# Softmax weights of the later head pairs: turned on VectorE before they go through DRAM

## The chip, the cores and the metric

One core of a Trainium2 chip. The metric is the device time of one execution in microseconds (us). Three executions of the kernel before took 894.09, 897.22 and 897.65 us (median 897.22). A fourth one was recorded by the profiler; it took 890.54 us, and all rows below are of it.

## The reference

Local and strided attention over 8 batches of 8 heads, 576 positions and 64 values a head, then layer norm and a two-layer network of width 512 and 2048:

```
mask_local   = (rel >= 0) & (rel < 32)                    # heads 0 to 3, rel = i - j
mask_strided = (rel >= 0) & (j % 32 == i % 32)            # heads 4 to 7
attn = softmax(where(mask, q k^T / 8, -1e9));   x = (attn v) as (8, 576, 512)
xn   = (x - mean) / sqrt(var + 1e-6) * g_ln
out  = x + relu(xn w_ch1) w_ch2
```

All of it is float32.

## The kernel before, in words

**Pairs.** Two heads of one batch are a pair; a batch has four pairs, by turns a local one (18 blocks of 32 queries against 64 keys) and a strided one (11 blocks of up to 54 positions that share a residue). Pairs are numbered 0 to 31: 0 to 7 are the first two batches, 8 to 11 the third. "Later pairs" are 8 to 31; of them 12 are local and 12 strided.

**The network.** Chunks of 512 tokens go through 16 steps each. A step is `ffn1` (12 products 512 wide into the bank `ph`, L800), then `hh` on ScalarE (L806) and `hl` on VectorE (L811), and `ffn2` of the step before (two halves of 6 products, L825). `ph` is one bank, so the next step's `ffn1` waits for `hl`. Steps are numbered n from 8 up; 8 to 23 are chunk 1, 24 to 31 the second half of chunk 0, from 32 on the other chunks.

**Attention between the steps.** A *visit* of pair i (`scores_and_values`, L611) stands between the network's products: on TensorE the values of pair i and then the scores of pair i+2, both in small tiles of the array (L656); on VectorE the scaling of the values into `xo` (L664), the mask and the row maximum; on GpSimd the subtraction (L485); on ScalarE the exponential (L490), which leaves the weights in `sm`. There is one `sm` for local and one for strided pairs. `x_store` then sends `xo` to DRAM. `sums` (L720) adds up the weights' rows on VectorE.

**Turning the weights.** The values need the weights transposed. Pairs 8 to 12 get that on TensorE: `turn_weights` (L701), 5 or 6 transposes of 128x128 and a copy by ScalarE. Pairs 13 to 31 get it by way of DRAM: `weights_out` (L676) stores `sm`, `weights_in` (L682) fetches it back through `to_blocks` (L696) in four transfers whose runs are 32 values long, and `turn_blocks` (L709) turns the 32x32 blocks on VectorE.

**Order.** All is issued in program order on each engine; SyncE issues nearly all transfers, in order. The start, until the first network steps run, is the hand-written list `ORDER`; there `K.n.w` is n idle products of width w on TensorE. From step 16 to 31 `early_steps` says by a letter and a pair what stands where: v visit, r sums, w turn_weights, o weights_out, p weights_in, x and y the fetching and turning of `x`, l the loading of v, t the turning of q and k, a and s rows of chunk 0. The fractions are places in a step: -0.25 ahead of `ffn1`, 0 after it, 0.25 between the halves of `ffn2`, 0.5 after them. From step 32 on the generator `visits` (L1097) does three parts for each pair, on three of every four steps.

Of the kernel before, what the change touches and what calls it, by code (L numbers as in the profile page):

```python
# [18 lines left out]

ORDER = """  # L20
L.a L.b L.c R.a/DVE L.X0 T.a K.1.512 K.1.256 L.Y0 R.b/POOL C.ka/ACT C.qa/DVE L.X1 T.b R.c/POOL S.a L.d C.qb/DVE
C.kb/ACT M.a w0.sc0 T.c w0.lo0 Z.a/DVE S.b K.1.256 C.qc/ACT L.va w0.mg0 U.a C.kc/ACT w0.sg0 M.b S.c w0.lo1 w0.bg
w0.sc1 Z.b/DVE E.a w0.mg1 U.b w1.sc0 L.vb P.a K.2.512 w0.sg1 M.c R.d/POOL w1.lo0 E.b w1.mg0 w0.cs T.d G.a w1.sg0
P.b w1.bg C.qd/DVE C.kd/ACT L.Y1 L.vc G.b Z.c/DVE w0.cm S.d w0.ce U.c V.a M.d L.X2 w0.hi0 w1.cs O.a E.c V.b L.Y2
w0.lw0 O.b w1.sc1 X.a w1.cm H.a L.a1 Z.d/DVE w1.lo1 X.b D.c/POOL Y.a H.b w1.mg1 P.c K.1.512 L.vd Y.b G.c U.d
w2.sc0 w1.sg1 w0.hi1 V.c w1.ce E.d w0.lw1 F1.0.b O.c w2.lo0 P.d L.b1 w2.sc1 w2.mg0 R.a1/POOL G.d X.c w2.sg0 H.c
K.1.512 T.a1 w2.lo1 w2.bg Y.c L.X3 w2.mg1 L.va1 C.ka1/ACT V.d w2.cs w2.sg1 F1.0.a C.qa1/ACT O.d w2.hi1 S.a1 L.Y3
w1.hi0 R.b1/POOL X.d M.a1 L.c1 w1.lw0 H.d Z.a1/DVE T.b1 U.a1 Y.d F1.1.b F1.1.a C.qb1/ACT C.kb1/DVE E.a1 w3.lo0
w3.sc0 D.a1/POOL F1.0.d w3.mg0 S.b1 w1.hi1 w3.sg0 w2.cm L.X4 P.a1 M.b1 w3.lo1 w3.bg F1.1.d L.vb1 G.a1 w2.ce
w3.cs w3.sc1 Z.b1/DVE V.a1 w2.hi0 w3.mg1 U.b1 F1.0.c O.a1 w3.cm F1.1.c w2.lw0 E.b1 L.Y4 w3.ce X.a1 L.X5 P.b1  # L30
# [13 lines left out]
def kernel(  # L44
# [14 lines left out]
    P = 128  # L59
# [132 lines left out]
    xd_l = [dram.tile([S, DM // 2], F32, name=f"xdl{b}") for b in range(B)]  # L192
    xd_s = [dram.tile([2 * NS * GS, DM // 2], F32, name=f"xds{b}") for b in range(B)]

    wd = [dram.tile([NS * P, P], F32, name=f"wd{i}") for i in range(2)]

    w1b, w2b = w1.bitcast(U32), w2.bitcast(U32)

# [412 lines left out]
    def scores_and_values(pv, p):  # L611

        one = p or pv
        n, last = one.nt, one.nt - 1
        slots = bank(f"sv{one.id}").rearrange("p (h r x) -> p h r x", h=2, x=SLOT)
        of_head = slots.shape[2]
        first_key = int(not one.local)
        vals = slots[:, :, n:2 * n] if pv else None
        keys = slots[:, :, first_key:first_key + last], slots[:, :, (first_key + last) % n]

        def middle(h, r):
            return of_head > CH // SLOT and (of_head * h + r) * SLOT // CH == 1

        passes = [[], []]
        places = [[] for _ in range(n)]
        for i, ((t, c), m) in enumerate(blocks(one)):
            places[t].append((i, c, m))
        for h in range(2):
            r = slice(64 * h, 64 * h + 64)
            if pv:  # L630
                rows = slice(64 * h, 64 * h + (64 if pv.local else GS))
                for t in sorted(range(n), key=lambda t: not middle(0, n + t)):
                    passes[h] += [
                        (vals[m * c:m * (c + 1), h, t], pv.pt[rows, t, m * c:m * (c + 1)],
                         pv.v[rows, i, 0:D], (64 * h, m * c), middle(h, n + t))
                        for i, c, m in places[t]]
            if p:
                w = 64 if p.local else GS
                step = STR if p.local else GS
                for t in sorted(range(n), key=lambda t: middle(1, (first_key + t) % n)):  # L640
                    to = keys[0][:, :, t] if t < last else keys[1]
                    passes[h] += [
                        (to[m * c:m * (c + 1), h, 0:w], p.qt[r, step * i:step * i + m],
                         p.kt[r, step * i:step * i + w], (64 * h, m * c),
                         middle(h, (first_key + t) % n))
                        for i, c, m in places[t]]
        written = [None, None]
        for both in zip(*passes):
            for h, (to, at, by, pos, shared) in enumerate(both):
                if shared and h and written[0] and not written[1]:  # L650
                    tc.add_manual_dep(
                        nc.tensor.nop().ins, written[0],
                        mybir.DependencyInfo(
                            mybir.DependencyClass.Sync, mybir.DependencyReason.DATA),
                        reason="both heads write the middle bank")
                ins = nc.tensor.matmul(  # L656
                    to, at, by, start=True, stop=True, tile_position=pos).ins
                if shared:
                    written[h] = ins.name
        if pv:  # L660
            xo = smp.tile([P, NS, 2, D], F32, tag="xo", name=f"xo{pv.id}")
            xot = xo.rearrange("p t h d -> p h t d")
            for rows, t0, t1 in ((P, 0, last), (64, last, n)):
                nc.vector.tensor_tensor(  # L664
                    out=xot[0:rows, :, t0:t1], in0=vals[0:rows, :, t0:t1],
                    in1=pv.den[0:rows, :, t0:t1].unsqueeze(3).broadcast_to([rows, 2, t1 - t0, D]),
                    op=ALU.mult)
            pv.xov = xo.rearrange("p t h d -> p t (h d)")
        if p:
            p.s_max(w, [(P, 0, last, keys[0][:, :, :, 0:w]),  # L670
                        (64, last, n, keys[1][0:64, :, 0:w].unsqueeze(2))])
            p.s_most(nc.vector.reduce_max)
            p.s_sub()
            p.s_act()

    def weights_out(p):  # L676

        nc.sync.dma_start(
            wd[int(p.local)].rearrange("(t p) x -> p t x", p=P)[:, 0:p.nt],
            p.sm[:, 0:p.nt].rearrange("p t h x -> p t (h x)"))  # L680

    def weights_in(p):  # L682

        p.pt = p.sm.rearrange("p t h x -> p t (h x)")
        p.sp = p.pt[:, 0:p.nt].rearrange("p t x -> p (t x)")
        to_blocks(p.sp, wd[int(p.local)][0:p.nt * P].rearrange("(j c) x -> c j x", c=32))

    def x_in(px):

# [8 lines left out]
            r = slice(32 * g, 32 * g + 32)  # L698
            nc.sync.dma_start(dst[r].rearrange("p (j e) -> p j e", e=32), src[:, :, r])

    def turn_weights(p):  # L701

        ps = bank(f"pp{p.id}")
        p.pt = p.sm.rearrange("p t h x -> p t (h x)")
        for t in range(p.nt):
            nc.tensor.transpose(ps[:, P * t:P * (t + 1)], p.pt[:, t], ident)  # L706
        nc.scalar.copy(out=p.pt[:, 0:p.nt].rearrange("p t x -> p (t x)"), in_=ps[:, 0:P * p.nt])

    def turn_blocks(px, p):  # L709

        if px:
            nc.vector.transpose(px.sx, px.sx)
            xh, xl = (t[:, px.h0 // 2, :] for t in x_t(px.b))
            nc.scalar.activation(out=xh, in_=px.sx, func=AF.Copy)
        if p:
            nc.vector.transpose(p.sp, p.sp)
        if px:
            nc.vector.tensor_tensor(out=xl, in0=px.sx, in1=xh.bitcast(F32), op=ALU.subtract)  # L718

    def sums(p):  # L720
        if p:
# [334 lines left out]
    def turn():  # L1056
        while todo:
            i = todo.pop()
            pairs[i].t_piece()
            if 2 * NHP <= i + 1 < NP:  # L1060
                pairs[i + 1].load_half(0)
                if i < 3 * NHP + 3:
                    pairs[i + 1].load_half(1)
# [4 lines left out]
    def visit(i):  # L1068
# [4 lines left out]
            turned(i + 3)  # L1073

    early_steps = {
# [5 lines left out]

    def early_step(n):
        stages = {"t": lambda p: p.t_piece(), "r": sums, "l": lambda p: p.load_v(), "x": x_in,
                  "w": turn_weights, "o": weights_out, "y": lambda p: turn_blocks(p, None), "p": weights_in}
        for word in early_steps.get(n, "").split():
            i = int(word[1:])
            if word[0] in "as":
# [9 lines left out]
    def visits():  # L1097

        for i in range(3 * NHP, NP):
            p, scored = pair(i + 1), pair(i + 2)  # L1100
            px = pairs[i] if pairs[i].b + 1 < B else None
            if p:
                weights_in(p)
            visit(i)
            if px:
                x_in(px)
            yield
            if i + 2 < NP:
                pairs[i + 2].load_v()
            yield  # L1110
            turn_blocks(px, p)
            sums(scored)
            if scored:
                weights_out(scored)
            if i + 4 < NP:
                pairs[i + 4].load_half(1, nc.scalar)
            yield

    late, two, h_last = {}, [], {}
    quarter = [slice(P * i, P * (i + 1)) for i in range(NT)]  # L1120
# [279 lines left out]
    for n, (r, f) in enumerate(steps):  # L1400
# [34 lines left out]
        early_step(n + 0.5)  # L1435
        if f == r.f0:
            prev[0].close()
        if old:
            old.column_mean()
            old.centred()  # L1440
# [80 lines left out]
```

## Time and profile before

| | before |
|---|---|
| median of three runs | 897.22 us (894.09 to 897.65) |
| profiled execution | 890.54 us, span 888.7 us |
| TensorE busy | 874.2 us (98%) |
| weight loads of TensorE | 715.2 us (80%) |
| VectorE, ScalarE, GpSimd busy | 454.2, 238.7, 238.5 us |
| granted TensorE clock, mean | 1.000 |

The profiled execution is 1.84 us longer than its span, which runs from the first instruction to the last. Matmuls overlap in the records: the distance of two starts is what one costs, not its duration.

### The profile page before, as it was taken

How to read it: one execution, taken by the hardware profiler on the slowest of the kernel's cores; microseconds unless marked ns; L12 is line 12 of the kernel's file. 1: busy time of each engine (PE TensorE's matmuls, PEld its weight loads, DVE VectorE, ACT ScalarE, POOL GpSimd, SP SyncE). 2: the span in 40 equal slices, each digit the busy share in tenths (PEclk: the TensorE clock that was granted, in tenths of full speed). 3: DMA queues.
4: the chain of work that ended last, by engine and by line, in shares of the span. 5: the costliest groups of instructions: out<-in, count | busy, mean ns of one | idle time of the engine just before them, and what ended most of it. 6: DMA issues, size and time to landing. Idle time of an engine off the chain costs nothing.

```text
span 888.7 us, 18483 instructions
## 1 busy us (share of the span) xinstructions
PE 874.2 (98%) x7425; PEld 715.2 (80%) x7425; DVE 454.2 (51%) x833; ACT 238.7 (27%) x431; POOL 238.5 (27%) x293
## 2 busy tenths in 40 slices
PE   7899999999999999999999999999999999999998
PEld 4678888888888888888888888878888788888886
DVE  5897476676554456445544555455543763333300
ACT  4765474212111111111111111111112543333200
POOL 6777286210000010000000000001000567676000
PEclk9999999999999999999999999999999999999999
DMA  9988880566676565657565657566532000001200
GB/s 212 227 200 249 215 247 1 123 143 148 117 165 123 103 128 132 118 100 126 129 137 113 119 106 155 112 122 129 140 91 80 13 32 28 1 1 46 95 26 24
DMA packets 339421, 101.70 MB, mean 114 GB/s; under 512 B 278160, under 2 KB 330248, under 8 KB 339336
## 3 DMA queue, kind: packets, MB, share of 16 engines
q1 hardware_dynamic: 300520, 95.28, 48.0%
q10 hardware_dynamic: 38816, 5.25, 3.6%
q8 instruction: 58, 0.95, 0.5%
q14 instruction: 27, 0.22, 0.1%
HBM read 73.42 MB, written 27.06 MB: 113 GB/s over the span
## 4 chain that ended last, share of the span: by engine, by line
PE 93%; DMA 4%; SPq 1%; DVE 1%; ACT 1%; issue 0%; POOL 0%; POOLq 0%; DVEq 0%; ACTq 0%
PE po L825 44%; PE ph L800 33%; PE u L1284 5%; PE sv L656 4%; PE v L1284 2%; DMA rows<-in_k_dram 2%; DMA v_l<-in_v_dram 1%; PE c L1284 1%; SPq L345 1%; DMA s<-in_moe_w_ch_dram 1%; SPq L356 0%; DMA v_s<-in_v_dram 0%; PE cm L267 0%; PE pp L706 0%; DVE xr L1151 0%
## 5 line engine op out<-in xcount | busy, mean ns | idle before, releaser
L825 PE MATMUL po<-w,hh 128*128 128x512 f32 x1024 | 320.5, 394 | 1.2 <-issue 0.8
L800 PE MATMUL ph<-xh,w 128*128 128x512 f32 x880 | 290.7, 391 | 0.0
L825 PEld LDWEIGHTS po<-w,hh 128*128 128x128 f32 x1024 | 189.1, 188 | 41.0 <-issue 1.0
L811 DVE SCALAR_TENSOR_TENSOR hl<-ph,hh 128x512 fp32r<-128x512 f32 x112 | 77.2, 690 | 257.5 <-ACT hh L806 257.2
L825 PE MATMUL po<-w,hl 128*128 128x512 f32 x512 | 199.6, 390 | 0.0
L800 PEld LDWEIGHTS ph<-xh,w 128*128 128x128 f32 x880 | 165.2, 188 | 34.2
L800 PE MATMUL ph<-xl,w 128*128 128x512 f32 x440 | 171.2, 389 | 0.0
L806 ACT ACTIVATE hh<-ph 128x512 fp32r<-128x512 f32 x112 | 66.7, 596 | 309.8 <-PE ph L800 284.4
L485 POOL TENSOR_TENSOR sm<-sm,mx 128x640 f32<-128x640 f32 (+1 forms) x32 | 40.6, 1269 | 343.6 <-DVE mx L481 331.8
L825 PEld LDWEIGHTS po<-w,hl 128*128 128x128 f32 x512 | 96.1, 188 | 20.7 <-issue 0.4
L800 PEld LDWEIGHTS ph<-xl,w 128*128 128x128 f32 x440 | 82.7, 188 | 16.9 <-DVE xl L718 0.2
L490 ACT ACTIVATE sm<-sm 128x640 f32<-128x640 f32 (+1 forms) x32 | 23.7, 742 | 125.3 <-POOL sm L485 125.3
L767 POOL TENSOR_TENSOR rs<-rs,mhalf 128x1 f32<-128x1 f32 x28 | 15.3, 549 | 100.8 <-DVE rs L766 94.5
L825 PE MATMUL po<-w,h 128*128 128x512 f32 x186 | 42.3, 389 | 0.0
L1151 POOL TENSOR_TENSOR sr<-sr,w 128x256 f32<-128x256 f32 x48 | 40.2, 838 | 3.8
L825 PEld LDWEIGHTS po<-w,h 128*128 128x128 f32 x186 | 34.9, 188 | 7.2
L1151 POOL TENSOR_TENSOR s<-sr,s 128x256 fp32r<-128x256 f32 x32 | 24.7, 799 | 25.5 <-ACT s L1270 25.5
L236 DVE SCALAR_TENSOR_TENSOR p<-s,p 128x512 uint32<-128x512 uint32 x32 | 22.0, 687 | 13.1 <-ACT p L232 11.2
L481 DVE TENSOR_REDUCE mx<-sm 128x10 f32<-128x640 f32 (+1 forms) x32 | 26.3, 823 | 1.9
L1151 DVE TENSOR_TENSOR x<-po,x 128x512 f32<-128x512 f32 x8 | 5.3, 688 | 39.6 <-PE po L825 29.9
L664 DVE TENSOR_TENSOR xo<-sv,den 64x128 f32<-64x128 f32 (+2 forms) x48 | 22.7, 515 | 4.5 <-PE sv L656 4.1
L566 DVE TENSOR_REDUCE den<-sm 128x10 f32<-128x640 f32 (+1 forms) x24 | 19.5, 811 | 7.8 <-ACT sm L490 7.8
(193 smaller groups left out, 974.2 us busy)
## 6 DMA issues: line engine op xcount, KB each, us to landing
s<-in_moe_w_ch_dram SPq DMA_DIRECT2D x32, 512.0 KB
out_dram<-x SPq DMA_DIRECT2D x32, 256.0 KB
raw<-in_q_dram SPq DMA_DIRECT2D x104, 72.0 KB
v_l<-in_v_dram SPq DMA_DIRECT2D x32, 144.0 KB
raw<-in_k_dram ACTq DMA_DIRECT2D x64, 72.0 KB
x<-xdl SPq DMA_DIRECT2D x34, 128.0 KB
x<-xds SPq DMA_DIRECT2D x34, 128.0 KB
xdl<-xo SPq DMA_DIRECT2D x16, 256.0 KB
```

Source lines behind the costliest of these rows:

```text
L236: nc.vector.scalar_tensor_tensor(out=self.p[i], in0=self.bits(i), scalar=3, in1=self.p[i], op0=ALU.logical_shift_left, op1=ALU.bitwise_or)
L481: engine(self.mx[:, :, 0:nt], self.smv, axis=AX.X)
L485: nc.gpsimd.tensor_tensor(out=sm, in0=sm, in1=mx[:, :, 0:nt].unsqueeze(3).broadcast_to([P, 2, nt, w]), op=ALU.subtract)
L490: nc.scalar.activation(out=self.smv, in_=self.smv, func=AF.Exp, scale=SCALE)
L656: ins = nc.tensor.matmul(to, at, by, start=True, stop=True, tile_position=pos).ins
L664: nc.vector.tensor_tensor(out=xot[0:rows, :, t0:t1], in0=vals[0:rows, :, t0:t1], in1=pv.den[0:rows, :, t0:t1].unsqueeze(3).broadcast_to([r ...
L800: nc.tensor.matmul(ph, w[:, cc], x[:, cc, :], start=(n + k == 0), stop=(n == NCC - 1 and k == 2))
L806: nc.scalar.activation(out=hh, in_=ph, func=AF.Relu)
L811: nc.vector.scalar_tensor_tensor(out=hl, in0=ph, scalar=0.0, in1=hh.bitcast(F32), op0=ALU.max, op1=ALU.subtract)
L825: nc.tensor.matmul(po, hx[:, cs], w, start=(start and n == 0), stop=(stop and n == 2))
L1151: engine.tensor_tensor(out=out, in0=a, in1=b, op=op)
L1284: nc.tensor.matmul(po, a[:, c], b[:, c, :], start=(start and c + k == 0), stop=(stop and c == 1 and k == 2), skip_group_check=True)
```

## The change

Pairs 8 to 12 no longer use TensorE for the turning; `turn_weights` is gone. All of 8 to 31 now do this: `weights_out` turns the 32x32 blocks on VectorE out of `sm` into a tile that shares the one buffer `xo` with the scaled values, and stores that tile in one transfer; `weights_in` fetches it in one transfer into `sm`, in four runs for each partition (160 values each for a local pair, 192 for a strided one). Nothing is turned after the fetch. In `sm` a strided pair's weights now lie 6 values (24 bytes) apart, a local pair's side by side as before. `early_steps` is written anew, with the loads of q and k of pairs 11 to 15 as steps of their own (q). In `visits` the sums and the store stand one part earlier. In `ORDER` some idle products are cut into narrower ones, and `K.2.256` is new.

```diff
-C.kb/ACT M.a w0.sc0 T.c w0.lo0 Z.a/DVE S.b K.1.256 C.qc/ACT L.va w0.mg0 U.a C.kc/ACT w0.sg0 M.b S.c w0.lo1 w0.bg
-w0.sc1 Z.b/DVE E.a w0.mg1 U.b w1.sc0 L.vb P.a K.2.512 w0.sg1 M.c R.d/POOL w1.lo0 E.b w1.mg0 w0.cs T.d G.a w1.sg0
-P.b w1.bg C.qd/DVE C.kd/ACT L.Y1 L.vc G.b Z.c/DVE w0.cm S.d w0.ce U.c V.a M.d L.X2 w0.hi0 w1.cs O.a E.c V.b L.Y2
+C.kb/ACT M.a w0.sc0 T.c w0.lo0 Z.a/DVE S.b K.2.128 C.qc/ACT L.va w0.mg0 U.a C.kc/ACT w0.sg0 M.b S.c w0.lo1 w0.bg
+w0.sc1 Z.b/DVE E.a w0.mg1 U.b w1.sc0 L.vb P.a K.8.128 w0.sg1 M.c R.d/POOL w1.lo0 E.b w1.mg0 w0.cs T.d G.a w1.sg0
+P.b K.2.256 w1.bg C.qd/DVE C.kd/ACT L.Y1 L.vc G.b Z.c/DVE w0.cm S.d w0.ce U.c V.a M.d L.X2 w0.hi0 w1.cs O.a E.c V.b L.Y2
...
-    wd = [dram.tile([NS * P, P], F32, name=f"wd{i}") for i in range(2)]
+    wd = [dram.tile([P, n * P], F32, name=f"wd{i}") for i, n in enumerate((NS, NL))]
...
-                        (vals[m * c:m * (c + 1), h, t], pv.pt[rows, t, m * c:m * (c + 1)],
+                        (vals[m * c:m * (c + 1), h, t], pv.pt[rows, t, c],
...
+    def blocks_out(to, flat, turned, src):
+        nc.vector.transpose(turned, src.rearrange("p t (i g) -> p g t i", g=4))
+        nc.sync.dma_start(to, flat)
+
+    def blocks_in(dst, src):
+        x = dst.shape[2]
+        nc.sync.dma_start(
+            dst, src.rearrange("p x -> (p x)").rearrange("(j c x) -> c j x", c=P, x=x))
+
     def weights_out(p):
-        nc.sync.dma_start(
-            wd[int(p.local)].rearrange("(t p) x -> p t x", p=P)[:, 0:p.nt],
-            p.sm[:, 0:p.nt].rearrange("p t h x -> p t (h x)"))
+        n = p.nt
+        t = smp.tile([P, NS, 2, D], F32, tag="xo", name=f"pw{p.id}")
+        t = t.rearrange("p t h d -> p (t h d)")[:, 0:P * n]
+        turned = (t.rearrange("p (g t e) -> p g t e", g=4, e=32) if p.local else
+                  t.rearrange("p (g e t) -> p g t e", g=4, e=32))
+        blocks_out(wd[int(p.local)], t, turned, p.sm[:, 0:n].rearrange("p t h x -> p t (h x)"))
 
     def weights_in(p):
-        p.pt = p.sm.rearrange("p t h x -> p t (h x)")
-        p.sp = p.pt[:, 0:p.nt].rearrange("p t x -> p (t x)")
-        to_blocks(p.sp, wd[int(p.local)][0:p.nt * P].rearrange("(j c) x -> c j x", c=32))
+        n = p.nt
+        sm = p.sm.rearrange("p t h x -> p (t h x)")[:, 0:P * n]
+        p.pt = (sm.rearrange("p (j t e) -> p t j e", j=4, e=32) if p.local else
+                sm.rearrange("p (c x t) -> p t c x", c=2, t=n))
+        blocks_in(sm.rearrange("p (j x) -> p j x", j=4), wd[int(p.local)])
...
-    def turn_weights(p):
-        ps = bank(f"pp{p.id}")
-        p.pt = p.sm.rearrange("p t h x -> p t (h x)")
-        for t in range(p.nt):
-            nc.tensor.transpose(ps[:, P * t:P * (t + 1)], p.pt[:, t], ident)
-        nc.scalar.copy(out=p.pt[:, 0:p.nt].rearrange("p t x -> p (t x)"), in_=ps[:, 0:P * p.nt])
...
-        if p:
-            nc.vector.transpose(p.sp, p.sp)
...
-            if 2 * NHP <= i + 1 < NP:
+            if 2 * NHP <= i + 1 < NP and not 10 < i + 1 < 16:
...
-        16: "t9", 17: "v6", 17.75: "r8", 18: "v7", 18.75: "r9", 19.25: "w8 a0", 20: "v8",
-        20.5: "a1", 20.75: "r10", 21: "x8", 21.25: "l10 s0", 21.5: "w9", 22.5: "s1", 23: "v9",
-        23.25: "a2", 23.75: "r11", 24.25: "l11", 24.75: "y8 x9", 25.25: "w10 a3", 26: "v10",
-        26.25: "s2", 26.5: "y9 x10", 27.25: "l12", 27.5: "w11 r12", 28.25: "s3", 29: "v11",
-        29.25: "y10", 29.5: "x11", 30.25: "l13", 30.5: "w12", 31: "r13 o13", 31.25: "y11"}
+        16: "t9", 17: "v6 o8", 18: "a0 v7", 18.25: "r8", 18.5: "p8", 18.75: "o9", 20: "q11",
+        20.25: "v8", 20.5: "r9", 20.75: "p9", 21.75: "r10 a1", 22: "x8", 22.25: "s0", 22.5: "o10",
+        22.75: "q12 l10", 23: "s1 v9", 23.5: "p10 a2", 25: "y8 o11", 25.25: "s2 q13", 25.75: "x9",
+        26: "v10", 26.25: "r11", 26.75: "l11", 27: "p11 y9", 27.25: "a3 x10", 28: "o12 q14",
+        28.25: "r12", 29: "y10 v11", 29.25: "p12 l12", 29.75: "x11", 30.75: "s3 q15", 31: "o13 y11",
+        31.25: "r13", 31.5: "l13"}
...
-            if i + 2 < NP:
-                pairs[i + 2].load_v()
+            if scored:
+                if i < NP - NHP - 1:
+                    weights_ready(scored)
+                    scored.load_v()
+                else:
+                    behind.append(scored)
             yield
-            turn_blocks(px, p)
-            sums(scored)
-            if scored:
-                weights_out(scored)
+            if px:
+                turn_blocks(px)
...
+    def weights_ready(p):
+        sums(p)
+        weights_out(p)
```

`behind` is emptied after the second half of `ffn2`; it holds the last few pairs only. Two further `K.1.512` of `ORDER` become `K.4.128`.

## Rows read from the trace of the kernel before

**Rows 1.** The page: span, and busy time, share and instructions of each engine.

```profile
span 888.7 us, 18483 instructions
PE 874.2 (98%) x7425; PEld 715.2 (80%) x7425; DVE 454.2 (51%) x833; ACT 238.7 (27%) x431; POOL 238.5 (27%) x293
```

**Rows 2.** Windows: stretch, its length, busy us of each engine, clock, DMA share, GB/s.

```profile
0.00:22.00 22.00, 17.12 (x248) 10.54 (x249) 12.30 (x38) 9.76 (x19) 15.12 (x40) 1.00 0.96 213
44.00:66.00 22.00, 20.43 (x328) 16.43 (x329) 19.62 (x36) 13.83 (x25) 16.32 (x17) 1.00 0.84 195
400.00:500.00 100.00, 100.00 (x875) 82.56 (x874) 48.24 (x88) 15.93 (x26) 7.27 (x8) 1.00 0.64 123
800.00:888.70 88.70, 84.78 (x380) 70.27 (x378) 19.22 (x29) 12.83 (x25) 13.49 (x17) 1.00 0.16 48
```

**Rows 3.** Chain that ended last, in order of time: start us, us, what.

```profile
161.38 2.72 PE ph L800 x12
164.10 1.37 PE po L825 x6
165.47 0.55 PE pp L706 x5
167.41 0.68 PE ph L800 x3
...
180.17 0.66 PE pp L706 x6
...
302.54 2.72 PE ph L800 x12
307.98 2.72 PE ph L800 x12
```

**Rows 4.** Line L706, the transposes: ns min/median/max, first and last start us.

```profile
L706 PE MATMUL pp<-ident,sm x27: 272/273/273, 165.3 to 236.8; 128*128 128x128 f32 x27
```

**Rows 5.** Weight loads of values: line L656, then TensorE's timeline of a strided visit.

```profile
L656 PEld LDWEIGHTS sv<-v_l,sm x864: 102/106/108, 170.1 to 649.9; 64*32 64x32 f32 x173
L656 PEld LDWEIGHTS sv<-v_s,sm x528: 129/135/136, 189.0 to 667.3; 54*64 54x64 f32 x176
316.06 0.78 PEld L656 LDWEIGHTS sv<-v_s,sm 54*64 54x64 f32 x44 [0.35 <-issue]
316.71 0.83 PEld L656 LDWEIGHTS sv<-kt_s,qt_s 64*64 64x64 f32 x44
```

**Rows 6.** VectorE's groups by line and shape: busy us, mean ns of one.

```profile
L811 DVE SCALAR_TENSOR_TENSOR hl<-ph,hh 128x512 fp32r<-128x512 f32 x112 | 77.2, 690 | 257.5 <-ACT hh L806 257.2
L236 DVE SCALAR_TENSOR_TENSOR p<-s,p 128x512 uint32<-128x512 uint32 x32 | 22.0, 687 | 13.1 <-ACT p L232 11.2 <-ACT s L226 1.9
L428 DVE STREAM_TRANSPOSE kt_s<-raw 128x576 f32<-128x576 f32 x13 | 16.1, 1241 | 0.0
L426 DVE STREAM_TRANSPOSE kt_l<-raw 128x576 f32<-128x576 f32 x13 | 9.6, 737 | 0.0
L716 DVE STREAM_TRANSPOSE sm<-sm 128x768 f32<-128x768 f32 x10 | 9.4, 942 | 0.0
```

**Rows 7.** VectorE's timeline, steps 18 and 19: start us, us, what, idle before.

```profile
158.43 0.82 DVE L566 TENSOR_REDUCE den<-sm 128x10 f32<-128x640 f32 x1 [2.14 <-ACT sm L490]
159.62 0.63 DVE L811 SCALAR_TENSOR_TENSOR hl<-ph,hh 128x512 fp32r<-128x512 f32 x1
164.08 0.83 DVE L566 TENSOR_REDUCE den<-sm 128x12 f32<-128x648 f32 x1 [2.17 <-ACT sm L490]
165.29 0.63 DVE L811 SCALAR_TENSOR_TENSOR hl<-ph,hh 128x512 fp32r<-128x512 f32 x1
```

**Rows 8.** Waits of SyncE's queue: us in total, times, longest us.

```profile
SPq L699 <- DMA wd<-sm: 67.9, 18, 5.7
```

**Rows 9.** TensorE's timeline in the start, around idle products (beats).

```profile
18.37 1.88 PE L915 MATMUL beats<-ident 128*128 128x512 f32 x4
20.93 1.09 PE L374 MATMUL t<-ident,flat 128*128 128x128 f32 x8 [0.68 <-POOL flat L368]
21.96 0.82 PE L495 MATMUL pp<-ident,sm 128*128 128x128 f32 x6
23.74 0.46 PE L267 MATMUL cm<-r,mean 128*128 128x128 f32 x2 [0.96 <-ACT kt_s L393]
```

More of the change, by code (lines that the diff above doesn't have):

```diff
@@ L21 @@
 L.a L.b L.c R.a/DVE L.X0 T.a K.1.512 K.1.256 L.Y0 R.b/POOL C.ka/ACT C.qa/DVE L.X1 T.b R.c/POOL S.a L.d C.qb/DVE
-C.kb/ACT M.a w0.sc0 T.c w0.lo0 Z.a/DVE S.b K.1.256 C.qc/ACT L.va w0.mg0 U.a C.kc/ACT w0.sg0 M.b S.c w0.lo1 w0.bg
-w0.sc1 Z.b/DVE E.a w0.mg1 U.b w1.sc0 L.vb P.a K.2.512 w0.sg1 M.c R.d/POOL w1.lo0 E.b w1.mg0 w0.cs T.d G.a w1.sg0
-P.b w1.bg C.qd/DVE C.kd/ACT L.Y1 L.vc G.b Z.c/DVE w0.cm S.d w0.ce U.c V.a M.d L.X2 w0.hi0 w1.cs O.a E.c V.b L.Y2
-w0.lw0 O.b w1.sc1 X.a w1.cm H.a L.a1 Z.d/DVE w1.lo1 X.b D.c/POOL Y.a H.b w1.mg1 P.c K.1.512 L.vd Y.b G.c U.d
+C.kb/ACT M.a w0.sc0 T.c w0.lo0 Z.a/DVE S.b K.2.128 C.qc/ACT L.va w0.mg0 U.a C.kc/ACT w0.sg0 M.b S.c w0.lo1 w0.bg
+w0.sc1 Z.b/DVE E.a w0.mg1 U.b w1.sc0 L.vb P.a K.8.128 w0.sg1 M.c R.d/POOL w1.lo0 E.b w1.mg0 w0.cs T.d G.a w1.sg0
+P.b K.2.256 w1.bg C.qd/DVE C.kd/ACT L.Y1 L.vc G.b Z.c/DVE w0.cm S.d w0.ce U.c V.a M.d L.X2 w0.hi0 w1.cs O.a E.c V.b L.Y2
+w0.lw0 O.b w1.sc1 X.a w1.cm H.a L.a1 Z.d/DVE w1.lo1 X.b D.c/POOL Y.a H.b w1.mg1 P.c K.4.128 L.vd Y.b G.c U.d
 w2.sc0 w1.sg1 w0.hi1 V.c w1.ce E.d w0.lw1 F1.0.b O.c w2.lo0 P.d L.b1 w2.sc1 w2.mg0 R.a1/POOL G.d X.c w2.sg0 H.c
-K.1.512 T.a1 w2.lo1 w2.bg Y.c L.X3 w2.mg1 L.va1 C.ka1/ACT V.d w2.cs w2.sg1 F1.0.a C.qa1/ACT O.d w2.hi1 S.a1 L.Y3
+K.4.128 T.a1 w2.lo1 w2.bg Y.c L.X3 w2.mg1 L.va1 C.ka1/ACT V.d w2.cs w2.sg1 F1.0.a C.qa1/ACT O.d w2.hi1 S.a1 L.Y3
 w1.hi0 R.b1/POOL X.d M.a1 L.c1 w1.lw0 H.d Z.a1/DVE T.b1 U.a1 Y.d F1.1.b F1.1.a C.qb1/ACT C.kb1/DVE E.a1 w3.lo0
@@ L699, in to_blocks, with turn_blocks @@
             nc.sync.dma_start(dst[r].rearrange("p (j e) -> p j e", e=32), src[:, :, r])
-    def turn_weights(p):
-        ps = bank(f"pp{p.id}")
-        p.pt = p.sm.rearrange("p t h x -> p t (h x)")
-        for t in range(p.nt):
-            nc.tensor.transpose(ps[:, P * t:P * (t + 1)], p.pt[:, t], ident)
-        nc.scalar.copy(out=p.pt[:, 0:p.nt].rearrange("p t x -> p (t x)"), in_=ps[:, 0:P * p.nt])
[L709 to L714, printed above, removed]
-        if p:
-            nc.vector.transpose(p.sp, p.sp)
-        if px:
-            nc.vector.tensor_tensor(out=xl, in0=px.sx, in1=xh.bitcast(F32), op=ALU.subtract)
+    def turn_blocks(px):
+        nc.vector.transpose(px.sx, px.sx)
+        xh, xl = (t[:, px.h0 // 2, :] for t in x_t(px.b))
+        nc.scalar.activation(out=xh, in_=px.sx, func=AF.Copy)
+        nc.vector.tensor_tensor(out=xl, in0=px.sx, in1=xh.bitcast(F32), op=ALU.subtract)
     def sums(p):
@@ L1075 @@
     early_steps = {
[5 rows of a table removed]
[6 rows of a table added]
     def early_step(n):
-        stages = {"t": lambda p: p.t_piece(), "r": sums, "l": lambda p: p.load_v(), "x": x_in,
-                  "w": turn_weights, "o": weights_out, "y": lambda p: turn_blocks(p, None), "p": weights_in}
+        stages = {"t": lambda p: p.t_piece(), "r": sums, "l": lambda p: p.load_v(), "x": x_in, "q": lambda p: p.load_qk(),
+                  "o": weights_out, "y": turn_blocks, "p": weights_in}
         for word in early_steps.get(n, "").split():
@@ L1107, in visits @@
             yield
-            if i + 2 < NP:
-                pairs[i + 2].load_v()
+            if scored:
[4 more added lines that the diff above has]
+                    behind.append(scored)
             yield
-            turn_blocks(px, p)
-            sums(scored)
-            if scored:
-                weights_out(scored)
+            if px:
+                turn_blocks(px)
             if i + 4 < NP:
                 pairs[i + 4].load_half(1, nc.scalar)
+            if scored and i >= NP - NHP - 1:
+                scored.load_v()
             yield
+    behind = []
+    def weights_ready(p):
+        sums(p)
+        weights_out(p)
     late, two, h_last = {}, [], {}
@@ L1437 @@
             prev[0].close()
+        while behind:
+            weights_ready(behind.pop())
         if old:
```

## The prediction

> **What bounds the kernel now.** I read the page's head first, then the windows, then the chain of waits in order of time. TensorE is busy for 874.2 of 888.7 us [rows 1]. The windows say where the other 14.5 us lie: 4.9 in the first 22 us, 1.6 between 44 and 66, 3.9 at the very end (after the last product come an addition and a store), and none at all from 400 to 500 us, with a granted clock of 1.00, the 2.4 GHz level [rows 2]. So from about 66 us on a saving counts only if it takes work off TensorE, and a loss counts as soon as it adds work there or makes it wait. VectorE is busy for 48 of the 100 us of that window, and the transfer engines are 0.64 busy at 123 GB/s without holding TensorE up; a lighter transfer is worth nothing there by itself. The reader is to see in the chain how regular it is: an ordinary step goes from 302.54 to 307.98, 5.44 us; the step that holds the transposes of pair 8 goes from 161.38 to 167.41, 6.03 us [rows 3].
>
> **The transposes.** 27 of 128x128 go [rows 4]: five each for pairs 8, 10, 12, six each for 9 and 11. Their records last 273 ns, 7.4 us in all, but they overlap; the chain gives five of them 0.55 us and six 0.66 us [rows 3]. 3 x 0.55 + 2 x 0.66 = 2.97 us, and the whole-step difference (0.59 instead of 0.55) adds 0.04 each: 3.2 us, of which I take 3.1. All of it lies in steps in which TensorE never waits, so it comes off the end in full: **-3.1 us**. ScalarE's five copies go as well and were hidden.
>
> **The weights 24 bytes apart.** This is the term that decides. For the 12 strided pairs TensorE now reads its stationary operand with 24 bytes from value to value, where it read them side by side. In a strided visit the 44 loads for the values start between 316.06 and 316.71, then those for the scores begin: 0.65 us, or 59 ns for each of the 11 loads that a quarter of the array gets one after another. A load of 32 columns takes 106 ns and one of 64 takes 135 [rows 5]: 29 ns for 32 columns, 58 ns for 64. The two numbers agree, so the stretch goes at the pace at which the columns are read, and a slower reading shows in full. No row has TensorE reading at a step. The nearest are VectorE's. Reading at a step of 8 bytes (the upper halves of 64-bit words, L236) takes 687 ns for 512 values, no more than the 690 of L811; writing at a step of 72 bytes (L428) takes 1241 ns where the same transpose written side by side takes 737 (L426), 1.69 times as long [rows 6]. So the factor is between 1 and 1.69 by these rows: 0 to 0.65 x 0.69 x 12 = 5.4 us. 24 bytes is three times the one step and a third of the other, so neither row is nearer by ratio; I take the middle, **+2.7 us**, and keep both ends. A gain is excluded, since a load can't get shorter by being spread out. The local pairs keep 32 values side by side: 0.
>
> The Trainium skill bears on this term (Advanced Engine Details and Errata, SBUF Cachelines): SBUF is read in lines of 16 bytes, two hits on a line are wanted to hide the access, and an access pattern that touches another line each time pays. At 24 bytes every value is in a line of its own, so by that rule the free end of my range is out; the rows of VectorE agree with it on both sides of 16 bytes, and none shows it for TensorE. The page has no figure for the penalty, so it gives no other sum; with the full 5.4 us in place of 2.7 the sum below would be 2.7 us higher.
>
> **VectorE's turning.** The 19 transposes of L716 (942 ns for a strided pair) become 24, read at a step of 16 bytes and for strided pairs written at 24: between 0.8 and 1.69 x 0.94 = 1.6 us each. VectorE has half its time free, and from step 32 on the turning stands two steps (10.9 us) behind the visit, its fetch two more steps later: 0. What queues behind it on VectorE is the next `hl`, due only with the next `ffn1`. SyncE's queue waited 67.9 us in 18 waits for stores of the weights [rows 8]; the earlier store takes most of these away, and nothing on TensorE hung on them: 0.
>
> **The early steps.** Here the turning is placed at once behind a visit (o8 at 17, o9 at 18.75), and VectorE must wait for the exponential with `hl` queued behind. In the trace of before it waits at the same place for the same thing: 2.14 us ahead of the sums of pair 8, with `hl` at 159.62, and 2.17 us ahead of those of pair 9, with `hl` at 165.29 [rows 7]. So the wait is not new; its work is replaced, 0.8 to 1.6 us of turning for 1.2 us of sums, which move behind the next visit. For pair 9 that gives: exponential done at 164.05, turning until 165.7, `hl` until about 166.4, while `ffn1` of step 20, moved up by the 0.59 us of the transposes, wants the bank at 166.8. It fits by 0.4 us: 0, and the cover is thin. The turned tile shares the single buffer `xo`, so turning pair 9 also waits until pair 8's store (issued at about 159.6) has landed; if that takes the longest wait of the queue, 5.7 us [rows 8], turning starts at 165.3, `hl` ends at 167.7, and TensorE loses 0.9 us. The fetch of pair 8 then starts at 165.3 as well and has until about 170.8, when the visit of step 20.25 needs it. The explicit loads of q and k stand two or more steps ahead of their turning: 0.
>
> **The start.** `K.2.256` is new: 512 columns. 1024 columns took 1.88 us, so it is 0.94 us long, behind the transposes that end at 22.78 and ahead of a product that in any case waits until 23.74, a hole of 0.96 us [rows 9]. The other four edits keep the columns and cut them up: 16 passes of 128 at the (1.09 - 0.27) / 7 = 0.117 us of the transposes beside them make 2.0 us where 1.88 stood, ahead of another hole of 0.68 us [rows 9]. I take 0; without the holes it would cost up to 0.94 + 0.3 = 1.2 us.
>
> **The sum.** -3.1 + 2.7 + 0 + 0 = -0.4 us: a profiled execution of 890.1 us after 890.54, with the same 1.8 us outside the span. The three timed runs have a median of 897.22, 6.7 us above the profiled one; what lies between them is in no row. I carry the difference over: 897.22 - 0.4 = 896.8, so 897 us, no change. For this kernel less than 0.5% (4.5 us) can't be told from no change. With the ends of the column term the forecast goes from 894 to 899.5; chance 0.55.
>
> **Rival 1, slower: the columns are read at half speed or less.** Place: the values of the 12 strided visits. Two quarters of the array read the same partitions at the same time; if readings that share nothing queue one behind another, the factor isn't VectorE's 1.69. At 2 it is +7.8 us, net +4.7, 902 us; at 4, both quarters in turn at half speed each, it is +23.4, net +20, 917 us. It decides from the point where 3.1 + 4.5 = 7.6 us are lost, a factor of 1.97. For it: the stretch goes at the pace of the loads. Against it: a step of 24 bytes is nearer to 16 than the 72 that gave 1.69, and a part of the loads may be hidden behind the products between them. Chance 0.23. The skill's rule named above speaks for this side too.
>
> **Rival 2: the early cover is gone.** One late `hl` or fetch costs about 0.9 us, and there are five early pairs: up to +4.5 us instead of 0, 897.7 to 901.5 us. For it: one buffer, and stores that took up to 5.7 us. Against it: the store is now in long runs, and only pairs 8 and 9 follow each other so closely. Chance 0.10.
>
> **Rival 3, faster: the idle products.** If the 6.7 us between the timed and the profiled executions are lost in the start, where TensorE has holes of 0.5 to 1.2 us, the filled holes may give some back: with the other terms as forecast down to 890 us. For it: the timed runs alone spread by 3.6 us. Against it: the profiled execution shows a granted clock of 1.00 in the first 22 us too [rows 2], so no row shows anything to be given back. Chance 0.12.
>
> **How the numbers follow.** Faster than 892.7: rival 3 with 0.10, and the low end of the forecast with the columns free, which at 894 is 1.4 us short of it, with 0.10: 0.20. Slower than 901.7: rival 1 with 0.20, rival 2 with 0.04, the upper end of the forecast with 0.06: 0.30. Same: 0.50. The range of 8 in 10 goes from 890.5, the end of rival 3, to 908, which takes in rival 1 up to a factor of 2.7 (-3.1 + 0.65 x 1.7 x 12 = +10.2).
>
> **What would show it.** No `pp` products and no copies of L707 after 160 us; steps 19 to 30 each shorter by 0.55 to 0.66 us where a transpose stood. In a strided visit, the distance from the first load of `v_s` to the first of `kt_s` in place of 0.65 us: 0.65 means that the columns are free (894 us), 0.87 is the forecast, 1.3 and more is rival 1; the median duration of these loads against 135 ns says the same. Local visits must stay as they are, or the layout is not the cause. Idle time of TensorE between 150 and 250 us, released by `hl` or by a fetch of `sm`, would be rival 2. A prediction that holds with none of these readings in place would be right by chance.

## The result, and the profile after

The changed kernel takes 900.02 us (median of 6 runs, 899.34 to 901.03); the kernel before, run beside it, takes 894.37 us (6 runs, 891.47 to 897.65). The ratio is 1.0073 with an interval of 1.0054 to 1.0092, so the change costs about 6.5 us (4.8 to 8.2). The forecast was 897 us and no change. Its base, the median of three runs, was itself high: 894.37 in these six runs and 892.5 to 893.2 in the later sets. In those sets 12 executions of the kernel before, with a mean granted clock of 0.993 to 0.996, took 895.1 to 897.9 us and the other 44, with 0.997 to 1.000, took 890.2 to 894.9; for the three runs of the base no clock is on record. What counts below is therefore the difference of 6.5 us against the -0.4 of the sum.

The profiled execution of the changed kernel took 899.37 us. Its page, beside [rows 1]:

```profile
span 897.2 us, 18417 instructions
PE 881.9 (98%) x7428; PEld 723.8 (81%) x7428; DVE 473.6 (53%) x838; ACT 235.1 (26%) x426; POOL 238.8 (27%) x293
```

The span has grown by 8.5 us and TensorE's busy time by 7.7. TensorE is busier with 27 transposes fewer, so what it still does has become longer. The windows (stretch, length, busy us of each engine, clock, DMA share, GB/s), the second beside [rows 2]:

```profile
145.00:250.00 105.00, 104.14 (x1126) 84.77 (x1125) 73.73 (x128) 19.45 (x32) 19.33 (x21) 1.00 0.69 150
400.00:500.00 100.00, 100.00 (x869) 82.70 (x868) 52.93 (x91) 15.29 (x25) 7.83 (x9) 1.00 0.58 116
```

From 400 to 500 us TensorE still never waits and the granted clock is 1.00, the 2.4 GHz level; from 145 to 250 us 0.86 us are idle, where the kernel before had none. TensorE's waits behind 145 us (line, what it waited for: us in total, times, longest) name who ended them; the one on `x` belongs to the end of the kernel:

```profile
PE px L795 <- ACT x L790: 0.8, 1, 0.8
PE ph L804 <- ACT xh L721: 0.4, 1, 0.4
PE ph L804 <- DVE hl L815: 0.2, 1, 0.2
PE ph L804 <- DVE xl L722: 0.2, 1, 0.2
```

The two chains show where the time is; `sv` are the products of a visit, `po` those of `ffn2`. First the chain of the kernel before (start us, us, what): a strided visit, a local one.

```profile
268.98 1.54 PE sv L656 x82
...
292.50 1.65 PE sv L656 x104
```

And that of the kernel after, at the same two visits:

```profile
271.28 2.21 PE sv L656 x82
...
295.52 1.65 PE sv L656 x106
```

The strided visit has grown from 1.54 to 2.21 us, the local one has stayed at 1.65. 0.67 us on each of 12 strided visits is 8.0 us. From the start of the one visit to the start of the next it is a little more: 292.50 - 268.98 = 23.52 us before and 295.52 - 271.28 = 24.24 after, 0.72 us or 8.6 for all 12, because the `ffn2` behind the visit is 0.05 us longer as well (2.99 instead of 2.94). The loads inside, by line (ns min/median/max, first and last start) and then in TensorE's timeline, answer to [rows 5]:

```profile
L656 PEld LDWEIGHTS sv<-v_l,sm x864: 102/106/107, 173.3 to 657.7; 64*32 64x32 f32 x173
L656 PEld LDWEIGHTS sv<-v_s,sm x528: 183/204/208, 190.1 to 675.7; 54*64 54x64 f32 x176
L656 PEld LDWEIGHTS sv<-kt_s,qt_s x528: 129/135/153, 160.0 to 640.2; 64*64 64x64 f32 x176
319.07 1.33 PEld L656 LDWEIGHTS sv<-v_s,sm 54*64 54x64 f32 x42 [0.35 <-issue]
320.28 0.14 PEld L656 LDWEIGHTS sv<-kt_s,qt_s 64*64 64x64 f32 x2
```

Only the loads that read the weights at 24 bytes have changed: 204 ns instead of 135. The distance from the first of them to the first load of `kt_s` is 320.28 - 319.07 = 1.21 us instead of 0.65, with two loads of the values still to come; with the 0.67 us by which the visit has grown it is 1.32, a factor of 2.0. The prediction had said what this reading would mean: 0.65 free, 0.87 the forecast, 1.3 the first rival. It had also said that the median load would say the same, and that was wrong: 204 / 135 is 1.5 only. By the prediction's own split 58 of the 135 ns are for reading 64 columns; if the other 77 stay, 127 are left of the 204, a factor of 2.2 (an estimate).

The other terms stand nearly as forecast. A step of the first early pairs has no transposes left; where [rows 3] had 6.03 us from `ph` to `ph` with `pp` between them, the chain after has 163.84 to 169.28, the 5.44 us of an ordinary step:

```profile
163.84 2.72 PE ph L804 x12
166.56 2.72 PE po L829 x12
169.28 2.72 PE ph L804 x12
```

VectorE's turning of a pair takes 1.25 to 1.64 us, inside the 0.8 to 1.6 of the prediction but for 0.04, and SyncE's queue waits for it about as long as it waited before for the stores [rows 8]; nothing on TensorE hangs on that wait:

```profile
L678 DVE STREAM_TRANSPOSE pw<-sm x24: 1251/1439/1641, 160.9 to 648.7; 128x640 f32<-128x640 f32 x12, 128x768 f32<-128x768 f32 x12
SPq L679 <- DVE pw L678: 66.4, 21, 9.4
```

The two profiles differ by +8.6 (strided visits) - 3.1 (transposes) + 0.9 (idle time after) - 0.8 (two waits of `po` in the kernel before, at 579 and 617 us, which the changed kernel hasn't) + 2.4 us in the start: the first products of step 17 begin at 148.27 before and at 150.71 after. That is 8.0 of 8.5. The last of these terms turned out to be the run's, not the change's (below).

### The profile page after: what moved, and what is told of

It reads as the page before. It is cut to its first block, busy times and chain, and to the rows that moved or that the text cites. A ratio compares the mean times of both kernels' runs of the same rounds, so it can differ in the third digit from the quotient of the medians.

```text
span 897.2 us, 18417 instructions
## 1 busy us (share of the span) xinstructions
PE 881.9 (98%) x7428; PEld 723.8 (81%) x7428; DVE 473.6 (53%) x838; ACT 235.1 (26%) x426; POOL 238.8 (27%) x293
## 4 chain that ended last, share of the span: by engine, by line
PE 85%; DMA 5%; SPq 4%; DVE 3%; ACT 1%; issue 1%; POOL 1%; DVEq 0%; POOLq 0%; ACTq 0%
PE po L829 40%; PE ph L804 30%; PE u L1299 5%; PE sv L656 5%; PE v L1299 2%; DMA s<-in_moe_w_ch_dram 1%; PE c L1299 1%; SPq L345 1%; DMA sx<-xdl 1%; DMA rows<-in_k_dram 1%; DMA v_l<-in_v_dram 1%; SPq L715 1%; SPq L356 0%; DMA sx<-xds 0%; SPq L360 0%
## 5 line engine op out<-in xcount | busy, mean ns | idle before, releaser
L678 DVE STREAM_TRANSPOSE pw<-sm 128x640 f32<-128x640 f32 (+1 forms) x24 | 34.2, 1424 | 2.7 <-ACT sm L490 2.7
```

The costliest lines, as they stand in the source:

```text
L678: nc.vector.transpose(turned, src.rearrange("p t (i g) -> p g t i", g=4))
```

## The experiments

The theory was that reading the weights 24 bytes apart costs TensorE 8 us and that the rest of the change is worth -1 to -3 us. The rivals were the start (the new beats), waits brought by the earlier turning, and a cost that grows with the step.

**The strided weights side by side again, in four transfers with runs of 32.**

```diff
-                  t.rearrange("p (g e t) -> p g t e", g=4, e=32))
+                  t.rearrange("p (g t e) -> p g t e", g=4, e=32))
...
+            for j in range(4):
+                nc.sync.dma_start(dst[:, j // 2, j % 2], src[j])
```

> The changed kernel, but a strided pair's weights lie side by side in sm again: they are fetched in four transfers with runs of 32 values instead of one with runs of 192; all else is as changed. Theory A (the 24-byte step in TensorE's weight loads costs 0.67 us in each of 12 strided visits, 8.0 us, and eats the 3.1 us of the transposes): the loads of v_s go back from 204 to 135 ns, the stretch of a strided visit from 1.24 to 0.65 us, and the time to 8.0 us below the changed kernel's 900.0, about 892, a little faster than before (ratio 0.997). Theory B (the new start or the new early steps lose the time): it stays at 898 to 900, ratio 1.004 or more.

Measured: 896.73 us, ratio 1.0042 (1.0021 to 1.0062). The loads are back at 129/135/135 ns, so the layout is the cause of the longer loads, but the kernel is still slower than before, where the theory expected 892. Its waits, a VectorE row of 231 us and SyncE's fetch of 221 us say what came instead:

```profile
PE po L835 <- issue: 3.4, 3, 1.7
PE ph L810 <- DVE hl L821: 3.2, 1, 3.2
231.71 0.71 DVE L725 STREAM_TRANSPOSE sx<-sx 128x512 f32<-128x512 f32 x1 [3.43 <-DMA sx<-xdl]
221.29 2.64 SPq L708 DMA_DIRECT2D sm<-wd x4
```

The four fetches hold SyncE for 2.64 us where one takes 0.39 us. The fetch of `x` for pair 10 stands behind them; VectorE waits 3.43 us for it, and the scaling, the mask and the maximum of the next visit queue behind it. So the exponential comes late on ScalarE (237.92 us), `hh` stands right behind it (238.57), and `hl` comes 3.2 us late for TensorE. The wait cost more than its own length here: up to 238 us the granted clock was 1.00, from 240 to 243 us, right after the wait, it was 0.50, the 1.2 GHz level, and from 244 us on 1.00 again, which by these windows is another 1.7 us (an estimate). The 3.4 us ahead of `po`, in which TensorE waited for nothing that the profile shows, are in some of the other profiles too, at changing places; what they are stays open. The experiment didn't isolate the step, so other ones had to.

**The old or the new order of the start.** The changed kernel with all of the old `ORDER`:

```diff
-C.kb/ACT M.a w0.sc0 T.c w0.lo0 Z.a/DVE S.b K.2.128 C.qc/ACT L.va w0.mg0 U.a C.kc/ACT w0.sg0 M.b S.c w0.lo1 w0.bg
+C.kb/ACT M.a w0.sc0 T.c w0.lo0 Z.a/DVE S.b K.1.256 C.qc/ACT L.va w0.mg0 U.a C.kc/ACT w0.sg0 M.b S.c w0.lo1 w0.bg
...
```

> The changed kernel with the list of the start as before (idle products of the old widths, without K.2.256). The profiled changed kernel reaches step 17 2.4 us later than the profiled kernel before. Theory A: the start is worth nothing, 900 as changed, within 1 us. Theory B: the 2.4 us come back, about 897.6, ratio to before 1.0036.

Measured: 900.23 us, ratio 1.0083 (1.0063 to 1.0104): the loss stays. The other way round, the kernel before with the new order alone:

> The kernel before with the changed list of the start alone (narrower idle products, K.2.256). Theory A: no change, ratio 1.000 within 0.002. Theory B: slower by 2.4 us, ratio 1.0027.

Measured: 892.91 us, ratio 1.0000 (0.9985 to 1.0016). The edits of the start are worth nothing. The first products of step 17 begin at 151.74 us in this profile, in the chain:

```profile
151.74 2.77 PE ph L800 x12
```

The nine other profiles, with the old start or the new, have them between 149.28 and 153.71 us; the profile of before, with 148.27, was the earliest. (In the latest one the granted clock was 0.84 between 44 and 66 us.)

**The step alone, on the kernel before.**

```diff
-                         (vals[m * c:m * (c + 1), h, t], pv.pt[rows, t, m * c:m * (c + 1)],
+                         (vals[m * c:m * (c + 1), h, t],
+                          pv.pt[rows, t, m * c:m * (c + 1)] if pv.local else apart(pv)[rows, t, c],
```

> The kernel before, in which the values of the 12 strided later pairs read their weights out of the same tile at a step of 24 bytes; nothing else is changed, and the weights read are not those that belong to the block. Theory A (the step costs 0.67 us in each of 12 visits): loads of v_s 204 ns instead of 135, 8.0 us slower than before, ratio 1.009. Theory C (the step costs only half of that, and the rest of the change's loss is stalls that its new steps bring): ratio 1.0045.

Measured: 901.26 us, ratio 1.0109 (1.0092 to 1.0127), 9.7 us (8.2 to 11.3). Nothing else is changed, the loads of the values show the same 204 ns, and the time is lost in full; from the strided visit to the local one behind it there are 24.23 us, as in the changed kernel. The 8.0 us of the visits alone lie just under the interval, the 8.6 us from start to start within it:

```profile
273.13 2.21 PE sv L660 x81
297.36 1.64 PE sv L660 x106
L660 PEld LDWEIGHTS sv<-v_s,sm x528: 183/204/213, 191.7 to 677.8; 54*64 54x64 f32 x176
```

**The change without the step.**

```diff
-                sm.rearrange("p (c x t) -> p t c x", c=2, t=n))
+                sm.rearrange("p (t c x) -> p t c x", c=2, t=n))
```

> The changed kernel, but a strided pair's weights are read side by side out of the same fetched tile, so that they are not those that belong to the block; transfers and steps are as changed. It is the first experiment without its four slow transfers. Theory A: 8.0 us off the changed kernel, ratio to before about 0.9985, with no more waits of TensorE than the 0.9 us that the changed kernel has between 145 and 250 us. Theory C: ratio 1.003.

Measured: 892.29 us, ratio 0.9991 (0.9976 to 1.0005). Without the step alone the whole loss is gone, and all the rest of the change together is worth -0.8 us (-2.1 to +0.4). Its loads, and its waits without the one at the end:

```profile
L656 PEld LDWEIGHTS sv<-v_s,sm x528: 129/135/135, 189.5 to 667.0; 54*64 54x64 f32 x176
PE ph L804 <- DVE hl L815: 0.8, 1, 0.8
PE ph L804 <- ACT xh L721: 0.3, 1, 0.3
PE ph L804 <- DVE xl L722: 0.2, 1, 0.2
```

**The transposes alone.** The kernel before without them:

```diff
-        ps = bank(f"pp{p.id}")
...
-        for t in range(p.nt):
-            nc.tensor.transpose(ps[:, P * t:P * (t + 1)], p.pt[:, t], ident)
-        nc.scalar.copy(out=p.pt[:, 0:p.nt].rearrange("p t x -> p (t x)"), in_=ps[:, 0:P * p.nt])
```

> The kernel before without the 27 transposes of pairs 8 to 12 and without ScalarE's copies; their weights stay as they are, so these pairs' values are of weights that are not turned. Both theories: 3.1 us faster, ratio 0.9965; if the transposes were hidden after all, 1.000.

Measured: 889.23 us, ratio 0.9969 (0.9957 to 0.9981), -2.8 us (-3.8 to -1.7): the -3.1 of the sum was right. Of it the 0.8, 0.3 and 0.2 us of the waits above are given back in the change without the step, and 0.2, 0.4 and 0.2 us in the full change.

**Eight steps in one kernel.** In the kernel before, the operands of the scores are read at 1, 2, 3, 4, 5, 6, 8 and 10 values' distance, one step per pair: q, the stationary operand with 64 columns, for strided pairs, and k, the moving one, for local pairs.

```diff
+                        return t[r, 0:m * apart].rearrange("p (x s) -> p x s", s=apart)[:, :, 0]
```

> The kernel before, in which the scores of the later pairs are made of other columns, at a step: in strided pairs TensorE's stationary operand (64 columns) and in local pairs its moving operand (64 columns) is read at a step of 1, 2, 3, 4, 5, 6, 8 or 10 values, one step for each pair, in turn; the true scores are left out. It shows what a load costs by its step. Theory A1 (what counts is how many lines of 16 bytes are touched): 135 ns at steps 1 and 2, more from 3 or 4 on, and no further growth beyond 4, 204 ns at 4 to 10. Rival A2 (any step costs): 204 ns from step 2 on. Rival A3 (the cost grows with the distance): 204 ns at 6, less at 4, over 220 at 10. For the moving operand there is no row yet: 216 ns at every step if it is read by a path with room, more from 4 on if not.

The loads of q at steps 1, 2, 3, 4, 5, 6, 8 and 10, in this order (ns min/median/max):

```profile
L665 PEld LDWEIGHTS sv<-kt_s,qt_s x44: 129/135/135, 324.9 to 325.6; 64*64 64x64 f32 x44
L665 PEld LDWEIGHTS sv<-kt_s,qt_s x44: 133/135/139, 372.1 to 372.9; 64*64 64x64 f32 x44
L665 PEld LDWEIGHTS sv<-kt_s,qt_s x44: 161/171/179, 419.5 to 420.5; 64*64 64x64 f32 x44
L665 PEld LDWEIGHTS sv<-kt_s,qt_s x44: 189/213/217, 467.4 to 468.8; 64*64 64x64 f32 x44
L665 PEld LDWEIGHTS sv<-kt_s,qt_s x44: 186/204/207, 515.7 to 517.0; 64*64 64x64 f32 x44
L665 PEld LDWEIGHTS sv<-kt_s,qt_s x44: 187/205/210, 563.9 to 565.2; 64*64 64x64 f32 x44
L665 PEld LDWEIGHTS sv<-kt_s,qt_s x44: 193/215/219, 607.0 to 608.4; 64*64 64x64 f32 x44
L665 PEld LDWEIGHTS sv<-kt_s,qt_s x44: 187/204/212, 644.5 to 645.8; 64*64 64x64 f32 x44
```

8 bytes are free, 12 cost about a half, and from 16 to 40 bytes all cost nearly the same, 204 to 215 ns. This is one profiled execution; at 24, 32 and 40 bytes a second pair of it shows 205, 214 and 204 ns. The stretch, read from the first and last start of the 44 loads, goes from 0.7 to 1.3 or 1.4 us. It is no price per byte of step. It fits a count of the values that share 16 bytes: at 8 bytes two do, at 12 two of every four, from 16 on none. That count is inferred from the staircase; no run moved where the first value lies or used values of another size. The products with k as the moving operand do the same: 216 ns at step 1, 218 at 2, 256 at 3, and 292 to 294 from 4 on, here at steps 1, 4 and 8:

```profile
L665 PE MATMUL sv<-kt_l,qt_l x72: 216/216/238, 301.4 to 302.2; 64*32 64x64 f32 x72
L665 PE MATMUL sv<-kt_l,qt_l x72: 274/292/305, 443.4 to 444.5; 64*32 64x64 f32 x72
L665 PE MATMUL sv<-kt_l,qt_l x72: 275/294/302, 588.2 to 589.3; 64*32 64x64 f32 x72
```

The Trainium skill's rule on this (Advanced Engine Details and Errata, SBUF Cachelines), lines of 16 bytes of which two hits each are wanted, fits this staircase: two values per line were free here, one per line was not. It gives no size; the runs gave it.

**Built on that: weights 8 bytes apart.** Two row groups are interleaved, so that the step is 2 values, with the four transfers in runs of 64; v11 stands ahead of y10.

```diff
+            turned = t.rearrange("p (g a e u) -> p g a u e", g=4, e=32, u=2)
...
+            for u in range(2):
+                nc.vector.transpose(turned[:, :, :, u], src[:, :, :, u])
...
-        28.25: "r12", 29: "y10 v11", 29.25: "p12 l12", 29.75: "x11", 30.75: "s3 q15", 31: "o13 y11",
+        28.25: "r12", 29: "v11", 29.25: "y10 x11", 29.5: "p12 l12", 30.75: "s3 q15", 31: "o13 y11",
```

> A version meant to win: the changed kernel with a strided pair's weights 8 bytes apart (two row groups interleaved), which cost nothing in the experiment with steps; fetched in four transfers with runs of 64 values; and at step 29 the visit of pair 11 ahead of the turning of x of pair 10, so that VectorE's wait for that fetch no longer stands ahead of the visit's scaling. Theory A: loads of v_s 135 ns, no wait for hl at step 30, 8.5 us off the changed kernel, ratio to before 0.997. Theory C: ratio above 1.002, with waits at other places.

Measured: 898.54 us, ratio 1.0060 (1.0045 to 1.0075): a miss. The loads are as hoped, but `hl` is late again. In order: loads, wait, VectorE's row, SyncE's rows.

```profile
L656 PEld LDWEIGHTS sv<-v_s,sm x528: 132/135/140, 193.1 to 676.7; 54*64 54x64 f32 x176
PE ph L816 <- DVE hl L827: 2.4, 1, 2.4
235.28 1.01 DVE L664 TENSOR_TENSOR xo<-sv,den 128x640 f32<-128x640 f32 x2 [4.10 <-DMA wd<-pw]
223.47 2.56 SPq L714 DMA_DIRECT2D sm<-wd x4
227.91 2.30 SPq L727 DMA_DIRECT2D sx<-xdl x4
230.31 1.46 SPq L679 DMA_DIRECT2D wd<-pw x1
```

VectorE waits 4.10 us to write `xo`, because pair 12's turned weights lie in the same single buffer and their store begins only at 230.31, behind p11's four transfers and x10's four. This is the mechanism of the prediction's second rival. As in the first experiment the granted clock falls to 0.50 right behind the wait, here from 243 to 245 us, another 1.7 us (an estimate from the clock of the windows). The rest of the loss isn't accounted for.

**Its store ahead of x10.**

```diff
-        26: "v10", 26.25: "r11", 26.75: "l11", 27: "p11 y9", 27.25: "a3 x10", 28: "o12 q14",
+        26: "v10", 26.25: "r11", 26.75: "l11", 27: "p11 y9", 27.25: "a3", 28: "o12 x10 q14",
```

> The version with weights 8 bytes apart, with one order on SyncE turned round: pair 12's store of its turned weights goes ahead of the fetch of x for pair 10. Theory A (in that version the store stood behind x10 and p11's transfers on SyncE, kept the xo buffer taken and so held back the product, VectorE and hl): the wait of ph on hl of 2.4 us in 200 to 250 is under 0.5, and the ratio to the kernel before falls from 1.006 to 1.003 or less. Theory B (the store's place on SyncE is not what held VectorE): a wait on hl of 2 us or more stays, and 1.006.

Measured: 898.98 us, ratio 1.0050 (1.0031 to 1.0070), between what the two theories expected. The wait on `hl` fell from 2.4 to 0.8 us, so the store's place did make it, but the total didn't follow (the intervals of the two versions overlap): the next store, pair 13's, is now the late one. First the waits, then VectorE and SyncE:

```profile
PE po L841 <- DVE x L909: 2.2, 1, 2.2
PE sv L656 <- DMA v_l<-in_v_dram: 1.2, 1, 1.2
PE ph L816 <- DVE hl L827: 0.8, 1, 0.8
253.63 0.88 DVE L664 TENSOR_TENSOR xo<-sv,den 128x512 f32<-128x512 f32 x2 [5.48 <-DMA wd<-pw]
249.34 0.44 SPq L700 DMA_DIRECT2D wd<-pw x1
```

VectorE stood 5.48 us for the one buffer, and the addition into `x` behind it came 2.2 us late for `po`. A buffer of its own for the turned weights, 3 KB per partition, wasn't tried.

**The local pairs alone.** Their 32 values stay side by side and one transfer fetches them; strided pairs go as before the change.

```diff
     def weights_out(p):
...
+        if not p.local:
+            nc.sync.dma_start(wd[0].rearrange("(t p) x -> p t x", p=P)[:, 0:n],
+                p.sm[:, 0:n].rearrange("p t h x -> p t (h x)"))
+            return
...
-        20.25: "v8", 20.5: "r9", 20.75: "p9", 21.75: "r10 a1", 22: "x8", 22.25: "s0", 22.5: "o10",
+        20.25: "v8", 20.5: "r9", 21.5: "w9", 21.75: "r10 a1", 22: "x8", 22.25: "s0", 22.5: "o10",
```

> The changed kernel with the local pairs' weights alone turned on VectorE ahead of their store; strided pairs' weights are handled as in the kernel before (pairs 9 and 11 turned on TensorE, from pair 13 on turned on VectorE behind a fetch in four transfers) and so read side by side. 15 of the 27 transposes stay out of TensorE, which is 15/27 of the 2.8 us that leaving out all was worth, 1.6 us. Theory A (the strided loads' lines are the whole of what the change loses): loads of v_s at 135 ns, strided visits back at 23.5 us, ratio to the kernel before 0.998, at most 1.000 if the local stores and fetches bring a wait of up to 1.6 us. Theory B (moving the turning ahead of the store is what costs, through VectorE's order and the one xo buffer, for local pairs as well): waits of ph or po on hl or xo of over 2 us in 200 to 300 us, and 1.002 or more.

Measured: 892.54 us, ratio 0.9987 (0.9972 to 1.0002). The loads are at 135 ns, and behind 145 us TensorE waits 0.6 us besides the wait at the end, none of it on `hl` or `xo`:

```profile
L656 PEld LDWEIGHTS sv<-v_s,sm x528: 129/135/135, 189.4 to 666.5; 54*64 54x64 f32 x176
PE px L815 <- ACT x L810: 0.8, 1, 0.8
PE sv L656 <- issue: 0.6, 1, 0.6
```

For local pairs the earlier turning doesn't hurt by itself. This is the best of the versions that compute all of it, but -1.2 us with an interval that reaches to no change isn't shown to be a gain.

## Why the prediction was wrong

**The step that failed** is the size of the term "the weights 24 bytes apart": +2.7 us was taken, between 0 and 5.4. It measures 8.0 us by the visits in the chain (12 of 0.67 us), 8.6 with the products behind them, and 9.7 (8.2 to 11.3) by itself. Two choices made it too small. The upper end, 1.69, was VectorE's; TensorE's factor is 2.0 by the visit. And the middle was taken because 24 bytes is as far from 8 as from 72 by ratio. That presumed a cost that rises with the step; the staircase shows that 16 bytes and 40 cost nearly alike, so 24 belonged wholly to the upper row. The sentence that set the two VectorE rows on both sides of 16 bytes had the answer, and the middle was taken against it. That 897 lies only 3 us from the 900.02 measured is luck: the base was some 3 to 5 us too high, which hid a good part of the missing cost.

**Rival 1 came true** in place and size: at a factor of 2 it had +7.8 for this term and 902 us. Its mechanism, two quarters of the array that read the same partitions and queue one behind another, is not shown: no run loads one quarter alone. The measured factor of 2.0 lies beyond its point of decision, 1.97, and the loss of 6.5 us beyond the 4.5 us that this point stood for; it is more than the rival's 4.7 because all the rest is worth -0.8 us and not the -3.1 of the transposes. The waits of 0.9 us explain a part of that; the interval of -0.8 is too wide to say more. The arguments against it both failed: nearness to 16 was no comfort, and nothing was hidden behind the products between the loads, as the loss of the whole 0.67 us per visit shows.

**What held:** the transposes (-2.8 measured, -3.1 predicted); the start at 0 (ratio 1.0000); VectorE's turning and SyncE's waits at 0, though these waits didn't go away as the prediction said (67.9 us before, 66.4 after); local visits unchanged. The early steps, put at 0, cost a little: idle time of TensorE with `hl` as its releaser in 145 to 250 us, which the prediction had named as the sign of Rival 2, is there with 0.2 us on `hl` and 0.86 in all. Their cover is as thin as was said: two versions with four fetches in place of one lose 2.4 and 3.2 us on `hl`. Rival 3 is out: the new beats alone give nothing.

**What the sum gives with the measured term:** +8.0 to 8.6 for the loads and -0.8 (-2.1 to +0.4) for all the rest is +7.2 to 7.8 us, within the 4.8 to 8.2 of the ratio.

## What to carry to other kernels

Before a layout is changed so that a transfer or a transpose goes away, look at how the engine that sets the end reads it: here, on a TensorE that hardly waits, the longer loads counted in full. A cost between two known steps isn't to be interpolated; ask at which size it changes, and measure both sides of it. A fetch cut into four takes four places on the queue that issues it, and a single buffer shared by two uses makes one use wait for the other's store. A wait can cost more than its length: look at the granted clock behind it.

## What the runs showed of the hardware

Reading 64 fp32 columns of the stationary operand took 135 ns at a step of 4 or 8 bytes, 171 at 12, and 204 to 215 from 16 to 40 bytes; the moving operand's products took 216 ns side by side and 292 to 294 at 16 and 32 bytes. Right behind waits of TensorE of 3.2 and 2.4 us the granted clock was 0.50, the 1.2 GHz level, where it had been 1.00; behind one of 2.2 us it stayed at 1.00. At 16 and 32 bytes the loads are 8 to 11 ns longer than at 20, 24 and 40. That was not expected and its cause wasn't tried, nor was that of TensorE's "issue" waits of 0.2 to 1.9 us at changing places.
